# Squared-ReLU attention and a two-layer MLP on one core: fewer and longer attention bursts between the MLP's matmuls

## Chip, core and metric

The kernel runs on one NeuronCore of a Trainium2 chip. The metric is the time of one execution on the device in microseconds. The profile is one execution taken by the hardware profiler. TensorE (PE) does the matrix products, ScalarE (ACT) and VectorE (DVE) read what it leaves in PSUM, GpSimd (POOL) casts inputs, SyncE (SP) issues most of the transfers.

## What is computed

There are 8 batches and 12 heads, with 448 rows and 64 columns per head. The inputs are float32.

```python
scores = (1 / sqrt(64)) * (q @ k.T)              # per batch and head
attn = maximum(scores, 0) ** 2 / 448
x = (attn @ v)  # heads side by side: 3584 rows of 768
h = x @ w_in                                      # 768 x 2048
g = maximum(h, 0) + alpha * minimum(h, 0)
out = g @ w_out                                   # 2048 x 768, float32
```

## The kernel before

**Quads and chunks.** The attention is cut into 24 quads, one for four heads of one batch: quads 3b to 3b+2 belong to batch b. The 448 keys of a quad are cut into 7 chunks (j = 0 to 6). For one chunk `scores` (L182) issues four matmuls on 64x64 tiles of the array, which run side by side, and a relu that takes the result from PSUM to a bf16 tile. `squares` (L206) or, for two chunks at a time in the first three quads, `squares2` (L196) squares it on VectorE. `attnv` (L218) multiplies the seven squared chunks of a quad by v, 28 matmuls on 64x64 tiles that add up in PSUM, and then copies the sum, scaled, to `xT`.

**MLP.** For each batch there are a first layer, `ffn1` (L255), of 16 units `ff`, six matmuls of 128x128 tiles each, and a second layer, `ffn2` (L273). A unit of the first layer is evacuated in two steps, `neg` on ScalarE (L269) and `gT` on VectorE (L270). A unit of the second layer is 16 matmuls in two halves, a copy on VectorE (L286), and for every second unit a store on SP's queue (L292). An even batch has 12 half units of the second layer, an odd one 16.

**PSUM.** `sc_ps` has two buffers of two banks for scores and A@V, `mm_ps` four of one bank, for the MLP, and for a burst's first chunk when it is given `mm_ps`.

**Order.** `manual_schedule` keeps the order in which the code issues instructions on each engine, so the written order is the schedule. Attention is not a stage of its own: while TensorE does the MLP of batch b, bursts of attention of later batches are put between its matmuls. Quads 0 to 2 come first; 3 to 5 are put by hand into batch 0's layers (the lists given to `play`, L468 to L476); 6 to 23 form one `stream` (L487) of chunks and A@V, cut into parts of three units, which `spread` (L345) puts at even distances between whole units of the first layer and half units of the second. `group` (L319) issues a part: A@V goes last, the first of three chunks uses `mm_ps` and either relus on ScalarE alone ("act2", in the first layer) or one half on each of ScalarE and VectorE ("both"). The A@V of a quad comes after chunk 1 of the next.

**Inputs.** With chunk 0 of quad n the group issues the loads of quad n+2 (`load`, L86) and the transposes of quad n+1 by DMA (`transpose`, L127), all on SP's queue; with chunk 4, the casts of quad n+2 to bf16 on POOL (`to_bf16`, L110). `raw`, `cast` and `qkT` have two buffers each, `o` three.

Of the kernel before, what the change touches and what calls it, by code (L numbers as in the profile page):

```python
# [20 lines left out]
NJ = 7  # L21
# [3 lines left out]
def kernel(  # L25
# [22 lines left out]
    def pool(name, bufs, **kw):  # L48
        return ctx.enter_context(tc.tile_pool(name=name, bufs=bufs, **kw))
# [5 lines left out]
    v_pool = pool("vp", 4)  # L55
    early_pool = pool("early", 2)
    qkT_pool = pool("qkT", 2)
    rl_pool = pool("rl", 3)
    at_pool = pool("at", 10)
    rl2_pool = pool("rl2", 3)  # L60
    at2_pool = pool("at2", 6)
    xT_pool = pool("xT", 2)
    g_pool = pool("g", 1)
    neg_pool = pool("neg", 3)
# [101 lines left out]
        else:  # L166
            nc.vector.tensor_scalar(rl[:, r], half[r][:, :S], 0.0, None, ALU.max)  # L167

    rl2, pairs = [], []

    def relu_tile(pair):

        if not pair:
            return rl_pool.tile([128, 2, S], BF16, tag="rl", name="rl")
        if not rl2:
            t = rl2_pool.tile([128, 2, 2, S], BF16, tag="rl2", name="rlp")
            rl2.extend([t, t])
            pairs.append(t)
        t = rl2.pop()
        return t[:, 1 - len(rl2)]  # L180

    def scores(n, j, relu="act", space=sc_ps, pair=False):  # L182

        ps, half = score_tile(space)
        score_mm(n, j, half)
        rl = relu_tile(pair)
        if relu in ("both", "act2"):
            relu_half(rl, half, 0, nc.scalar)
            relu_half(rl, half, 1, nc.vector if relu == "both" else nc.scalar)
        elif relu == "dve":  # L190
            nc.vector.tensor_scalar(rl, ps[:, :, :S], 0.0, None, ALU.max)
        else:
            nc.scalar.activation(rl, ps[:, :, :S], ACTF.Relu)  # L193
        todo.append((n, j, rl))

    def squares2(keep=0):  # L196

        while len(todo) >= 2 + keep:
            two = [todo.pop(0) for _ in range(2)]
            t = pairs.pop(0)  # L200
            a = at2_pool.tile([128, 2, 2, S], BF16, tag="at2", name="atp")
            nc.vector.tensor_tensor(a, t, t, ALU.mult)  # L202
            for i, (n, j, _) in enumerate(two):
                att[(n, j)] = a[:, i]

    def squares(keep=0, eng=None):  # L206
        while len(todo) > keep:
            n, j, rl = todo.pop(0)
            a = at_pool.tile([128, 2, S], BF16, tag="at", name="at")
            if eng is nc.scalar:  # L210
                nc.scalar.activation(a, rl, ACTF.Square)
            else:
                nc.vector.tensor_tensor(a, rl, rl, ALU.mult)  # L213
            att[(n, j)] = a

    av_ps = {}

    def attnv(n, js=range(NJ), space=sc_ps, apart=False):  # L218
        b, g = quads[n]
        if js[0] == 0:  # L220
            if space is mm_ps:
                av_ps[n] = [mm_ps.tile([128, 512], F32, tag="mm", name="avh") for _ in range(2)]
            elif apart:
                av_ps[n] = [sc_ps.tile([128, 2, 512], F32, tag="sc", name="av2")[:, 0] for _ in range(2)]
            else:
                av_ps[n] = sc_ps.tile([128, 2, 512], F32, tag="sc", name="av")
        ps = av_ps[n]
        half = ps if isinstance(ps, list) else [ps[:, r] for r in range(2)]
        for j in js:
            a = att.pop((n, j))  # L230
            for r in range(2):
                for s in range(2):
                    nc.tensor.matmul(half[r][64 * s:64 * s + 64, :S],  # L233
                                     vb[n][64 * r:64 * r + 64, s, j, :],
                                     a[64 * r:64 * r + 64, s],
                                     start=(j == 0), stop=(j == NJ - 1))
        if js[-1] != NJ - 1:
            return
        if g == 0:
            xT[b] = xT_pool.tile([128, NG, 2, S], BF16, tag="xT", name="xT")  # L240
        if b == 0:
            nc.scalar.activation(xT[b][:, g, 0], half[0][:, :S], ACTF.Copy, scale=out_scale)
            if g > 0:
                nc.vector.tensor_scalar(xT[b][:, g, 1], half[1][:, :S], out_scale, None, ALU.mult)
            else:
                nc.scalar.activation(xT[b][:, g, 1], half[1][:, :S], ACTF.Copy, scale=out_scale)
        else:
            nc.scalar.activation(xT[b][:, g], ps[:, :, :S], ACTF.Copy, scale=out_scale)  # L248

# [69 lines left out]
    def group(units, how="both"):  # L319

        def f():
            order = sorted(units, key=lambda u: u[1] == "av")
            for i, (n, j) in enumerate(order):
                if j == "av":
                    attnv(n)
                elif i == 0 and len(order) == 3:
                    scores(n, j, how, mm_ps)
                else:
                    scores(n, j)
            squares()  # L330
            for n, j in order:
                if n < n_pe:
                    continue
                if j == 0:
                    if n + 2 < NQ:
                        load(n + 2)
                    if n + 1 < NQ:
                        transpose(n + 1, "k")
                        transpose(n + 1, "q")
                if j == 4 and n > 2 * NG and n + 2 < NQ:  # L340
                    for w in "kqv":
                        to_bf16(n + 2, w, nc.gpsimd)
        return f

    def spread(seq, items, share=0.92):  # L345

        total = sum(x[0] for x in seq) * share
        done, n = 0.0, 0
        for cost, fn in seq:
            while n < len(items) and done >= total * n / len(items):  # L350
                items[n]()
                n += 1
            fn()
            done += cost
        assert n == len(items)


    warm_w = singles.tile([128, 128], BF16)
# [34 lines left out]
    transpose(0, "k", first, nc.scalar)  # L393
    warm(2)
    nc.vector.tensor_copy(cast[(0, "k")][:, :, 3:], raw[(0, "k")][:, :, 3:])
    scores(0, 0, pair=True)
    scores(0, 1, pair=True)
    scores(0, 2, "both", mm_ps, pair=True)
    transpose(0, "k", rest)
    ps = mm_ps.tile([128, KF], F32, tag="mm", name="aps")  # L400
    nc.tensor.transpose(ps, alpha_sb, ident_f)
    nc.vector.tensor_scalar(beta_sb, ps, -1.0, 1.0, ALU.mult, ALU.add)
    squares2(keep=1)
    for n in range(NG):
        last = n == NG - 1
        for j in range(NJ):
            if n == 0 and j < 3:
                continue
            if last and j == 6:
                scores(n, j)  # L410
                squares2()
            elif j == 5 and not last or j == 2:
                scores(n, j, "both", mm_ps, pair=True)
            else:
                scores(n, j, "dve" if last and j == 4 else "act", pair=True)
            if not (last and j == 6):
                squares2(keep=1)
            if j == 2 and n > 0:
                attnv(n - 1, space=mm_ps)
            if j == 3 and not last:  # L420
# [17 lines left out]
    nc.gpsimd.dma_start(out=w_out_sb[:, :, :384], in_=w_out_v[:, :, :384])  # L438
    load_bf16(4)
    nc.gpsimd.dma_start(out=w_out_sb[:, :, 384:], in_=w_out_v[:, :, 384:])  # L440
    squares(eng=nc.scalar)
    attnv(2, range(0, 4), apart=True)
    attnv(2, range(4, NJ))
    ffn1(0, 3, range(0, 4))
# [12 lines left out]
    def play(seq):  # L457
        for x in seq:
            x()

    def g(*units):
        return group([(int(u[0]), "av" if u[1:] == "a" else int(u[1:])) for u in units])


    for ff in range(4):
# [5 lines left out]
    load(6, after=w_out_sb[:, 0, 384:385])  # L471
    load(7)
    o = [lambda c=c, hf=hf, h=h: ffn2(0, c, hf, h) for hf in range(2) for c in range(3) for h in range(2)]
    play([g("36"), turn(4), o[0], o[1], g("40", "41", "3a"), o[2], o[3], g("42", "43", "44"), o[4], o[5],
          g("45", "46"), o[6], turn(5), o[7], g("50", "51", "4a"), feed(6, "k", "q"), o[8], o[9],
          g("52", "53", "54"), feed(6, "v"), o[10], g("55", "56"), feed(7, "k", "q"), o[11]])  # L476

    ffn1(1, 0, range(0, 4))
    ffn1(1, 1, range(0, 4))
# [4 lines left out]
        ffn1(1, ff, range(4, KM))  # L484


    stream = []  # L487
    for n in range(2 * NG, NQ):
        for j in range(NJ):
            stream.append((n, j))  # L490
            if j == 1 and n > 2 * NG:
                stream.append((n - 1, "av"))
    stream.append((NQ - 1, "av"))
    parts = [stream[:2]] + [stream[i:i + 3] for i in range(2, len(stream), 3)]

    count = 0
    for b in range(1, B - 1):
        n_in, n_out = ((2, 7 if b == 1 else 6) if b % 2 else (3, 5))
        if b == B - 2:
            n_out = len(parts) - count - n_in  # L500
        mlp = steps(b, "in")
        bursts = [group(x, "act2") for x in parts[count:count + n_in]]
        if b == 1:
            bursts.append(lambda: [to_bf16(2 * NG + 2, w, nc.gpsimd) for w in "kqv"])
        spread(mlp[3:] if b == 1 else mlp, bursts, 0.95)
        count += n_in
        spread(steps(b, "out"), [group(x) for x in parts[count:count + n_out]], 0.92)
        count += n_out
    for _, fn in steps(B - 1, "in") + steps(B - 1, "out")[:-4]:
        fn()  # L510
    ffn2_last(B // 2 - 1, NJ - 1)
# [30 lines left out]
```

## Time and profile before

| | us |
|---|---|
| median of 9 runs | 396.9 (396.08 to 398.68) |
| the profiled execution | 396.34 |
| its span, first to last instruction | 394.5 |
| TensorE busy with matmuls | 384.0 |
| VectorE busy | 256.5 |
| ScalarE busy | 220.4 |
| GpSimd busy | 71.9 |
| mean granted clock of TensorE | 0.996 |

Two kinds of lines of the profile are used below. A line of a group has: kernel line, engine, operation, tiles (out<-in) with shapes, count | busy us, mean ns of one | idle time before it and what ended it. A line of the timeline has: start in us from the begin of the span, time to the end of the last of the merged instructions, engine, kernel line, operation, tiles and count. The end of a matmul in it is modelled and laps over the start of the next, so rates are read from start to start. In square brackets stands idle time of the engine ahead of the line and what ended it.

### The profile page before, as it was taken

What the parts mean: (1) busy time and instruction counts of PE and PEld (TensorE: products, weight loads), DVE (VectorE), ACT (ScalarE), POOL (GpSimd) and SP (SyncE); (2) the same over time, 40 slices, a digit from 0 to 9 for tenths busy, and PEclk for the clock granted to TensorE, in tenths of its full rate; (3) what the DMA queues carried; (4) which work ended last, traced back from release to release, by engine and by line L of the source; (5) the groups of instructions that cost most, each with busy time, mean ns of one, the idle gap of its engine ahead of it and who ended that gap; (6) DMA issues with size and microseconds to landing.
All of it is one profiled execution on the core that took longest, in us unless ns stands there. A gap on an engine that the chain in (4) does not pass through costs nothing.

```text
span 394.5 us, 7951 instructions
## 1 busy us (share of the span) xinstructions
PE 384.0 (97%) x3210; PEld 201.6 (51%) x3210; DVE 256.5 (65%) x406; ACT 220.4 (56%) x345; POOL 71.9 (18%) x88
## 2 busy tenths in 40 slices
PE   6799999999999999999999999999999999999996
PEld 4344555445555455544555455554555545555564
DVE  3966965676675877577664877667575776735421
ACT  5966847674655674466553765646454575624200
POOL 5654000022031430042020350033002300000000
PEclk9989999999999999999999999999999999999999
DMA  7999998592579923492097962295058720130033
GB/s 158 181 209 204 205 216 274 128 310 37 150 132 213 298 86 88 123 284 47 2 218 216 252 178 47 75 265 154 2 155 177 206 47 2 42 80 2 0 81 80
DMA packets 64756, 55.44 MB, mean 141 GB/s; under 512 B 35776, under 2 KB 60496, under 8 KB 64720
## 3 DMA queue, kind: packets, MB, share of 16 engines
q1 hardware_dynamic: 53472, 44.77, 44.8%
q0 software_dynamic: 10976, 9.96, 15.9%
q8 instruction: 25, 0.41, 0.4%
q10 hardware_dynamic: 272, 0.21, 0.2%
q14 instruction: 11, 0.09, 0.1%
HBM read 45.62 MB, written 11.01 MB: 144 GB/s over the span
## 4 chain that ended last, share of the span: by engine, by line
PE 92%; DVE 3%; ACT 2%; DMA 1%; issue 1%; ACTq 0%; DVEq 0%
PE ops L278 36%; PE hps L262 36%; PE av L233 8%; PE sc L158 5%; PE sch L158 4%; PE ops L301 1%; DVE atp L202 1%; ACT rlp L193 1%; DMA qraw<-in_q_dram 1%; PE tps L133 1%; DVE at L213 1%; PE avh L233 1%; ACT rl L193 0%; DVE gT L270 0%; ACT xT L248 0%
## 5 line engine op out<-in xcount | busy, mean ns | idle before, releaser
L262 PE MATMUL hps<-xT,w_in_sb 128*128 128x448 bf16 x768 | 150.1, 353 | 0.5 <-DVE gT L270 0.2
L278 PE MATMUL ops<-w_out_sb,gT 128*128 128x384 bf16 x864 | 147.9, 327 | 0.0
L278 PEld LDWEIGHTS <-gT 128*128 128x128 bf16 x864 | 81.1, 98 | 64.9 <-issue 14.2
L262 PEld LDWEIGHTS <-w_in_sb 128*128 128x128 bf16 x768 | 73.2, 98 | 74.5 <-issue 8.9
L213 DVE TENSOR_TENSOR at<-rl 128x896 bf16<-128x896 bf16 x147 | 97.8, 684 | 18.1 <-ACT rl L193 7.6
L270 DVE SCALAR_TENSOR_TENSOR gT<-neg,beta_sb,hps 128x448 bf16<-128x448 f32 x128 | 84.0, 677 | 36.7 <-ACT neg L269 36.5
L269 ACT ACTIVATE neg<-hps 128x448 f32<-128x448 f32 x128 | 68.5, 553 | 56.6 <-PE hps L262 54.5
L193 ACT ACTIVATE rl<-sc 128x896 bf16<-128x896 f32 x95 | 83.3, 926 | 1.7 <-PE sc L158 1.7
L165 ACT ACTIVATE rl<-sch 128x448 bf16<-128x448 f32 x67 | 34.8, 543 | 76.2 <-PE sch L158 76.2
L286 DVE COPY osb<-ops 128x384 f32<-128x384 f32 x54 | 30.0, 555 | 51.5 <-PE ops L278 51.5
L108 POOL CAST kb<-kraw 128x896 bf16<-128x896 f32 x16 | 16.5, 1031 | 207.2 <-DMA kraw<-in_k_dram 199.8
L158 PE MATMUL sc<-qT,kT 64*64 64x448 bf16 x440 | 33.8, 354 | 3.5 <-ACT rlp L193 1.8
L167 DVE TENSOR_SCALAR rl<-sch 128x448 bf16<-128x448 f32 x39 | 24.2, 621 | 15.4 <-PE sch L158 15.4
L233 PE MATMUL av<-at,vb 64*64 64x448 bf16 x592 | 32.0, 349 | 0.0
L158 PEld LDWEIGHTS <-kT 64*64 64x64 bf16 x672 | 14.9, 106 | 28.5 <-issue 22.5
L233 PEld LDWEIGHTS <-vb 64*64 64x64 bf16 x672 | 20.7, 110 | 13.8 <-issue 1.8
L248 ACT ACTIVATE xT<-av 128x896 bf16<-128x896 f32 x21 | 19.4, 922 | 7.4 <-PE av L233 7.3
L158 PE MATMUL sch<-qT,kT 64*64 64x448 bf16 x232 | 22.5, 376 | 0.0
L108 POOL CAST vb<-vraw 128x896 bf16<-128x896 f32 x16 | 17.4, 1089 | 0.0
L108 POOL CAST qb<-qraw 128x896 bf16<-128x896 f32 x16 | 17.4, 1085 | 0.0
L193 ACT ACTIVATE rlp<-sc 128x896 bf16<-128x896 f32 x14 | 12.3, 931 | 1.2 <-PE sc L158 1.2
L202 DVE TENSOR_TENSOR atp<-rlp 128x1792 bf16<-128x1792 bf16 x10 | 10.8, 1089 | 0.7 <-ACT rlp L193 0.3
(56 smaller groups left out, 87.9 us busy)
## 6 DMA issues: line engine op xcount, KB each, us to landing
out_dram<-osb SPq DMA_DIRECT2D x54, 192.0 KB, 2.8
qraw<-in_q_dram SPq DMA_DIRECT2D x19, 448.0 KB, 4.6
kraw<-in_k_dram SPq DMA_DIRECT2D x18, 448.0 KB, 5.4
vraw<-in_v_dram SPq DMA_DIRECT2D x18, 448.0 KB, 6.2
w_out_sb<-in_moe_w_out_dram POOLq DMA_DIRECT2D x2, 1536.0 KB, 21.2
w_in_sb<-in_moe_w_in_dram POOLq DMA_DIRECT2D x8, 192.0 KB, 8.5
w_in_sb<-in_moe_w_in_dram POOLq DMA_DIRECT2D x4, 384.0 KB, 9.9
vb<-in_v_dram POOLq DMA_DIRECT2D x6, 224.0 KB, 9.3
```

The costliest lines, as they stand in the source:

```text
L108: eng.tensor_copy(o, i)
L158: nc.tensor.matmul(half[r][64 * c:64 * c + 64, :S], kT[n][64 * r:64 * r + 64, j, c, :], qT[n][64 * r:64 * r + 64, :, c, :], start=True, st ...
L165: nc.scalar.activation(rl[:, r], half[r][:, :S], ACTF.Relu)
L167: nc.vector.tensor_scalar(rl[:, r], half[r][:, :S], 0.0, None, ALU.max)
L193: nc.scalar.activation(rl, ps[:, :, :S], ACTF.Relu)
L213: nc.vector.tensor_tensor(a, rl, rl, ALU.mult)
L233: nc.tensor.matmul(half[r][64 * s:64 * s + 64, :S], vb[n][64 * r:64 * r + 64, s, j, :], a[64 * r:64 * r + 64, s], start=(j == 0), stop=(j ...
L262: nc.tensor.matmul(ps, w_in_sb[:, km // 2, km % 2, bass.ts(ff, 128)], xT[b][:, km // 2, km % 2, :], start=(km == 0), stop=(km == KM - 1))
L269: nc.scalar.activation(neg, ps, ACTF.Relu, scale=-1.0)
L270: nc.vector.scalar_tensor_tensor(gT[b // 2][:, ff, (b % 2) * S:(b % 2) * S + S], neg, beta_sb[:, ff:ff + 1], ps, ALU.mult, ALU.add)
L278: nc.tensor.matmul(ps, gT[sb][:, ff, bass.ts(c, 128)], w_out_sb[:, ff, bass.ts(hf, 384)], start=(ff == 0), stop=(ff == KF - 1))
L286: nc.vector.tensor_copy(o[:, bass.ts(hf, 384)], ps)
```

## The change

For quads 6 to 23, `stream`, `parts` and `spread` are replaced by two bursts for each quad at written-out steps: `first_half` has chunks 0 to 2, `second_half` chunks 3 and 4, the A@V of the preceding quad on two `mm_ps` banks, and chunks 5 and 6. The steps count half units: in the first layer 32 of three matmuls (a burst at an odd step stands inside the accumulation of a unit), and then those of the second layer from step 32 on. Quad 6 has its chunks 3 to 6 in two bursts of two (`two`). For quads 3 to 5 the list behind `o` gets groups of three and two `wrap`s (two chunks, A@V, two chunks). All squares are of two chunks at a time, on tiles of `rl` (four buffers) and `at` (eight), but for the last chunk of a quad or stage. The sum of an A@V on `mm_ps` goes half to ScalarE and half to VectorE. `feed_next` issues the casts of quad n+1 and its transposes after the first half of quad n, and the loads of n+2 stay with that half.

```diff
-    def squares(keep=0, eng=None):
-        while len(todo) > keep:
...
+    def squares(keep=0, single=None):
+        while len(todo) >= 2 + keep or todo and single is not None:
+            m = min(len(todo), 2)
+            some = [todo.pop(0) for _ in range(m)]
+            t = some[0][2]
+            a = at_pool.tile([128, 2, 2, S], BF16, tag="at", name="at")
+            if m == 2:
+                nc.vector.tensor_tensor(a, t, t, ALU.mult)
...
+        elif isinstance(ps, list):
+            nc.scalar.activation(xT[b][:, g, 0], half[0][:, :S], ACTF.Copy, scale=out_scale)
+            nc.vector.tensor_scalar(xT[b][:, g, 1], half[1][:, :S], out_scale, None, ALU.mult)
...
+    def wrap(before, n, after):
+        def f():
+            scores(n + 1, before, "act")
+            scores(n + 1, before + 1, "dve")
+            attnv(n, space=mm_ps)
+            scores(n + 1, after, "act")
+            scores(n + 1, after + 1, "act")
+            squares()
+        return f
...
-    play([g("36"), turn(4), o[0], o[1], g("40", "41", "3a"), o[2], o[3], g("42", "43", "44"), o[4], o[5],
-          g("45", "46"), o[6], turn(5), o[7], g("50", "51", "4a"), feed(6, "k", "q"), o[8], o[9],
-          g("52", "53", "54"), feed(6, "v"), o[10], g("55", "56"), feed(7, "k", "q"), o[11]])
+    play([o[0], turn(4), o[1], g("36", "40", "41"), o[2], o[3], wrap(2, 3, 4), o[4], turn(5), o[5],
+          g("46", "50", "51"), o[6], o[7], wrap(2, 4, 4), feed(6, "k", "q"), o[8], o[9], g("56"), flush, feed(6, "v"), feed(7, "k", "q"), o[10], o[11]])
...
+    def first_half(n):
+        scores(n, 0, "act2", mm_ps)
+        scores(n, 1, "dve")
+        scores(n, 2, "act")
+        squares()
+        if n + 2 < NQ:
+            load(n + 2)
+        if n == 2 * NG:
+            transpose(n + 1, "k")
+            transpose(n + 1, "q")
+
+    def second_half(n):
+        scores(n, 3, "act")
+        scores(n, 4, "dve")
+        attnv(n - 1, space=mm_ps)
+        scores(n, 5, "act")
+        scores(n, 6, "act")
+        squares(keep=1)
...
+    def feed_next(n, w):
+        if n + 1 < NQ:
+            to_bf16(n + 1, w, nc.vector if w == None else nc.scalar if w == None else nc.gpsimd)
+            if w != "v":
+                transpose(n + 1, w)
...
+    STEPS = {1: [9, 17, 25, 33, 36, 38, 41, 43, 46], 0: [9, 23, 33, 35, 38, 41], 2: [9, 23, 33, 36, 40, 44]}
     for b in range(1, B - 1):
...
+        lo, hi = (2 * NG if b == 1 else 3 * b + 4), min(3 * b + 7, NQ)
+        where = STEPS[1] if b == 1 else STEPS[2 * (b % 2)]
+        items = [(n, f) for n in range(lo, hi) for f in (first_half, second_half)]
+        if b == 1:
+            items[1:2] = [(2 * NG, two(2 * NG, 3)), (2 * NG, two(2 * NG, 5, True))]
...
+            if f is first_half and n > 2 * NG:
+                for d, w in zip((2,4,6) if s < 32 else (0,0,1), "kqv"):
+                    at.setdefault(s + d, []).append(lambda n=n, w=w: feed_next(n, w))
+            if f is second_half:
+                for d, sq in zip((3,5) if s < 32 else (0,0), (squares, flush)):
+                    at.setdefault(s + d, []).append(sq)
         if b == B - 2:
+            at.setdefault(where[len(items)], []).append(lambda: attnv(NQ - 1))
```

More of the change, by code (lines that the diff above doesn't have):

```diff
@@ L57 @@
     qkT_pool = pool("qkT", 2)
[L58 to L61, printed above, removed]
+    rl_pool = pool("rl", 4)
+    at_pool = pool("at", 8)
     xT_pool = pool("xT", 2)
@@ L167, in relu_half, with scores @@
             nc.vector.tensor_scalar(rl[:, r], half[r][:, :S], 0.0, None, ALU.max)
[L169 to L182, printed above, removed]
-        ps, half = score_tile(space)
-        score_mm(n, j, half)
-        rl = relu_tile(pair)
+    cur = []
+    def scores(n, j, relu="act", space=sc_ps, rs=range(2)):
+        ps, half = score_tile(space)
+        score_mm(n, j, half, rs)
+        if cur:
+            t, i = cur.pop(), 1
+        else:
+            t, i = rl_pool.tile([128, 2, 2, S], BF16, tag="rl", name="rl"), 0
+            cur.append(t)
+        rl = t[:, i]
         if relu in ("both", "act2"):
@@ L193, in scores @@
             nc.scalar.activation(rl, ps[:, :, :S], ACTF.Relu)
[L194 to L203, printed above, removed]
-                att[(n, j)] = a[:, i]
-    def squares(keep=0, eng=None):
-        while len(todo) > keep:
[L208 to L214, printed above, removed]
+        todo.append((n, j, t))
+    def squares(keep=0, single=None):
[6 more added lines that the diff above has]
+                nc.vector.tensor_tensor(a, t, t, ALU.mult)
+            else:
+                cur.clear()
+                if single is nc.scalar:
+                    nc.scalar.activation(a[:, 0], t[:, 0], ACTF.Square)
+                else:
+                    nc.vector.tensor_tensor(a[:, 0], t[:, 0], t[:, 0], ALU.mult)
+            for i, (n, j, _) in enumerate(some):
+                att[(n, j)] = a[:, i]
     av_ps = {}
@@ L324, in f @@
                 if j == "av":
+                    if (n, NJ - 1) not in att:
+                        squares(single=nc.vector)
                     attnv(n)
@@ L343, in group @@
         return f
[L345 to L355, printed above, removed]
     warm_w = singles.tile([128, 128], BF16)
@@ L395 @@
     nc.vector.tensor_copy(cast[(0, "k")][:, :, 3:], raw[(0, "k")][:, :, 3:])
-    scores(0, 0, pair=True)
-    scores(0, 1, pair=True)
-    scores(0, 2, "both", mm_ps, pair=True)
+    scores(0, 0)
+    scores(0, 1)
+    scores(0, 2, "both", mm_ps)
     transpose(0, "k", rest)
@@ L402 @@
     nc.vector.tensor_scalar(beta_sb, ps, -1.0, 1.0, ALU.mult, ALU.add)
-    squares2(keep=1)
+    squares(keep=1)
     for n in range(NG):
@@ L410 @@
                 scores(n, j)
-                squares2()
+                squares()
             elif j == 5 and not last or j == 2:
-                scores(n, j, "both", mm_ps, pair=True)
+                scores(n, j, "both", mm_ps)
             else:
-                scores(n, j, "dve" if last and j == 4 else "act", pair=True)
+                scores(n, j, "dve" if last and j == 4 else "act")
             if not (last and j == 6):
-                squares2(keep=1)
+                squares(keep=1)
             if j == 2 and n > 0:
@@ L440 @@
     nc.gpsimd.dma_start(out=w_out_sb[:, :, 384:], in_=w_out_v[:, :, 384:])
-    squares(eng=nc.scalar)
+    squares(single=nc.scalar)
     attnv(2, range(0, 4), apart=True)
@@ L459, in play, with flush @@
             x()
+    def wrap(before, n, after):
[7 more added lines that the diff above has]
+        return f
     def g(*units):
         return group([(int(u[0]), "av" if u[1:] == "a" else int(u[1:])) for u in units])
+    def flush():
+        squares(single=nc.vector)
     for ff in range(4):
@@ L484 @@
         ffn1(1, ff, range(4, KM))
[L487 to L496, printed above, removed]
-    for b in range(1, B - 1):
-        n_in, n_out = ((2, 7 if b == 1 else 6) if b % 2 else (3, 5))
-        if b == B - 2:
[L500 to L508, printed above, removed]
+    def first_half(n):
+        scores(n, 0, "act2", mm_ps)
+        scores(n, 1, "dve")
+        scores(n, 2, "act")
+        squares()
+        if n + 2 < NQ:
[3 more added lines that the diff above has]
+            transpose(n + 1, "q")
@@ new lines, in second_half, with two, f @@
+    def second_half(n):
[4 more added lines that the diff above has]
+        scores(n, 6, "act")
+        squares(keep=1)
+    def two(n, j, last=False):
+        def f():
+            scores(n, j, "act2", mm_ps)
+            scores(n, j + 1, "act")
+            if last:
+                flush()
+            else:
+                squares()
+        return f
+    def feed_next(n, w):
[3 more added lines that the diff above has]
+                transpose(n + 1, w)
@@ new lines, in mlp_steps @@
+    def mlp_steps(b):
+        seq = [(0.56, h == 1, lambda ff=ff, h=h: ffn1(b, ff, range(3 * h, 3 * h + 3))) for ff in range(KF) for h in range(2)]
+        return seq + [(1.3, True, fn) for _, fn in steps(b, "out")]
+    STEPS = {1: [9, 17, 25, 33, 36, 38, 41, 43, 46], 0: [9, 23, 33, 35, 38, 41], 2: [9, 23, 33, 36, 40, 44]}
+    for b in range(1, B - 1):
+        mlp = mlp_steps(b)
+        at = {}
+        lo, hi = (2 * NG if b == 1 else 3 * b + 4), min(3 * b + 7, NQ)
[3 more added lines that the diff above has]
+            items[1:2] = [(2 * NG, two(2 * NG, 3)), (2 * NG, two(2 * NG, 5, True))]
+        for (n, f), s in zip(items, where):
+            at.setdefault(s, []).append(lambda n=n, f=f: f(n) if f in (first_half, second_half) else f())
+            if f is first_half and n > 2 * NG:
[4 more added lines that the diff above has]
+                    at.setdefault(s + d, []).append(sq)
+        if b == B - 2:
+            at.setdefault(where[len(items)], []).append(lambda: attnv(NQ - 1))
+        for i, (_, _, fn) in enumerate(mlp):
+            for x in at.pop(i, []):
+                x()
+            if b > 1 or i >= 6:
+                fn()
+        assert not at, at
```

## The prediction, made before the changed kernel ran

> **What bounds the kernel now.** I read the page's busy shares first, then the chain that ended last, then TensorE alone in order of time.
>
> ```profile
> PE 384.0 (97%) x3210; PEld 201.6 (51%) x3210; DVE 256.5 (65%) x406; ACT 220.4 (56%) x345; POOL 71.9 (18%) x88
> PE 92%; DVE 3%; ACT 2%; DMA 1%; issue 1%; ACTq 0%; DVEq 0%
> ```
>
> TensorE is busy 97% of the span and 92% of the last chain is its own work, with a granted clock of 0.996. An edit that leaves TensorE's instruction list alone can therefore gain only by the time between instructions. The timeline of TensorE shows where that is:
>
> ```profile
> 202.71 2.77 PE L278 MATMUL ops<-w_out_sb,gT 128*128 128x384 bf16 x16
> 205.41 0.38 PE L158 MATMUL sch<-qT,kT 64*64 64x448 bf16 x4
> 205.63 0.55 PE L158 MATMUL sc<-qT,kT 64*64 64x448 bf16 x8
> 206.11 4.07 PE L278 MATMUL ops<-w_out_sb,gT 128*128 128x384 bf16 x24
> 210.11 0.38 PE L158 MATMUL sch<-qT,kT 64*64 64x448 bf16 x4
> ```
>
> Column one is the start. 16 MLP matmuls take 205.41 - 202.71 = 2.70 us to the next start, 24 take 210.11 - 206.11 = 4.00: 0.1625 us each, and 0.10 us that is not matmul, at the edge into attention. The burst of three score chunks takes 206.11 - 205.41 = 0.70 us, where a further chunk costs 0.19 (205.63 to 206.11 holds two and the way out, and the seven chunks of an A@V run at the same 0.19): 3 x 0.19 = 0.57, so 0.13 us more. A burst of attention between MLP matmuls so costs **0.23 us** beside its work, whatever its length: the price of going from 128x128 to 64x64 tiles and back. It is no idle time in the profile; the modelled ends of the matmuls cover it.
>
> **The rule beside the row.** The Trainium skill's TensorEngine Tiling (Array Packing), Key Properties, says that changing the tiling mode drains TensorE, and gives no price; its TensorE: Matmul & The Clock Gate, Single matmul latency, puts the part of a warm matmul that isn't streaming at about 0.166 us. Two drains by that estimate are 0.33 us a burst; the trace has 0.23. I take the row. With 13 bursts fewer (below) the page would give -4.3 us and the row -3.0.
>
> **The change, part by part.**
>
> *Bursts.* Before, the written-out stream of quads 6 to 23 has 18 x 7 chunks and 18 A@V, 144 units: one part of 2 and 48 of up to 3, 49 bursts, which is what the timeline shows from 77.7 us on. After, STEPS places 9 bursts for batch 1, 6 in each of batches 2 to 5, 4 in batch 6 and one for the last A@V: 9 + 24 + 4 + 1 = 38. In the hand-made order of quads 3 to 5 behind `o`, score and A@V bursts go from 8 (four groups of three units, two of two, chunk 36 and the last A@V) to 6: two groups of three, two `wrap`s, chunk 56, the last A@V. The two `turn`s stay. 13 bursts x 0.23 = **-3.0 us**, all on the path. Matmuls and weights loaded are the same number.
>
> *A stall that goes.* In the stretch of quad 5, chunk 56 waits for a score buffer, since the cast of quad 6's v sits on ScalarE ahead of a relu:
>
> ```profile
> 70.52 0.95 ACT L106 CAST vb<-vraw 128x896 bf16<-128x896 f32 x1
> 70.70 0.38 PE L158 MATMUL sc<-qT,kT 64*64 64x448 bf16 x4 [0.15 <-ACT rl L193]
> ```
>
> Its start is 0.53 us after the chunk before it instead of 0.18. After, chunk 56 is alone and both buffers are free: **-0.35 us**. The wait for xT of quad 5 behind its A@V at 76 us stays.
>
> *Evacuation.* Squares: before 147 single ones and 10 pairs on VectorE; after 74 pairs and 19 singles.
>
> ```profile
> L213 DVE TENSOR_TENSOR at<-rl 128x896 bf16<-128x896 bf16 x147 | 97.8, 684 | 18.1 <-ACT rl L193 7.6
> L202 DVE TENSOR_TENSOR atp<-rlp 128x1792 bf16<-128x1792 bf16 x10 | 10.8, 1089 | 0.7 <-ACT rlp L193 0.3
> L191 DVE TENSOR_SCALAR rlp<-sc 128x896 bf16<-128x896 f32 x1 | 1.1, 1081 | 0.0
> ```
>
> 147 x 0.684 + 10 x 1.089 = 111.4 us becomes 74 x 1.089 + 19 x 0.684 = 93.6: -17.8. Relus: 39 half tiles at 0.621 leave VectorE, 4 of those stay, and 37 whole ones at 1.081 come (chunks 1 and 4 of the late quads, one per `wrap`): +18. Nineteen halves of xT at 0.62 come: +12. VectorE ends 12 us up, near 269 of 391 us; ScalarE loses some 28 us of its instructions. Both lie beside TensorE; this costs nothing as long as the burst doesn't wait for a PSUM buffer. That cover has to be worked out, for the Tiling page's PSUM Bottleneck speaks against the change: tiling speeds TensorE, not the evacuation, and the copies may become the bound. The paces, from a burst in the first MLP layer:
>
> ```profile
> 269.37 0.38 PE L158 MATMUL sch<-qT,kT 64*64 64x448 bf16 x4
> 269.48 0.54 ACT L269 ACTIVATE neg<-hps 128x448 f32<-128x448 f32 x1 [0.59 <-PE hps L262]
> 269.92 0.98 ACT L165 ACTIVATE rl<-sch 128x448 bf16<-128x448 f32 x2
> 270.06 0.68 DVE L270 SCALAR_TENSOR_TENSOR gT<-neg,beta_sb,hps 128x448 bf16<-128x448 f32 x1 [0.45 <-ACT neg L269]
> 270.77 1.75 ACT L193 ACTIVATE rl<-sc 128x896 bf16<-128x896 f32 x2
> ```
>
> ScalarE starts half tiles 0.44 us apart and whole ones 0.82; VectorE frees the last MLP bank 1.37 us after a burst begins (270.06 + 0.68 - 269.37). The new bursts of the first layer stand at odd steps, three matmuls (0.57 us) after the last full unit, so that one is free at 0.80.
>
> Second half at step 23, times from its first score: chunk 3 at 0, chunk 4 at 0.21, A@V 0.40 to 1.73, chunk 5 at 1.73, chunk 6 at 1.92, MLP again at 2.2. ScalarE: relu 3 0.42-1.35, half of xT 1.95-2.49, relus 5 and 6 to 4.1, then `neg` of the broken-off unit ff 11, 4.0-4.5. VectorE: gT of ff 10 to 0.80, relu 4 0.72-1.80, half of xT to 2.57, two pairs to 4.7, gT of ff 11 to 5.3. So chunk 5 has its buffer 0.35 us early and chunk 6 with about 0.06 us to spare (0.05 us from release to TensorE taken off): **0**, and 0.1 to 0.3 a burst if relu 4 is late. In the second layer VectorE has only a copy of 0.56 us ahead, and relu 4 starts at 0.65: more room. MLP banks: ff 12 (2.77) takes ff 10's (0.80), ff 13 (3.91) and ff 14 (5.04) the two of the A@V (2.5, 2.6), ff 15 (6.18) that of ff 11 (5.3): 0.9 us of room. First half at step 9: MLP again at 0.69; ff 5 to ff 7 take banks free at 0.80, 0.96 and 1.4, ff 8 (4.67) that of ff 4 (gT at 3.6): 1 us of room. This holds because the pool gives the bank that was freed first: in the compiled program of before, after the burst at 316.11 us ff 6 has ff 4's bank, ff 7 the first score half's, and only ff 8 that of ff 5.
>
> I add **+0.3 us** for waits that this leaves, chiefly at the first burst of quad 6, close behind three units that finish together; its bounds are 0 and 2. Below nothing is excluded.
>
> *Queues.* `feed_next` casts quad n+1 on POOL and issues its two transposes on SP behind the loads of n+2; before, the casts came with chunk 4, for n+2. No instruction is added. SP's order stays loads, transposes, stores.
>
> ```profile
> kT<-kb SPq DMA_TRANSPOSE x18, 5.5
> qT<-qb SPq DMA_TRANSPOSE x18, 4.8
> ```
>
> A transpose waits for the last score of the quad two back, and a store behind it on SP waits with it. The tightest case is quad 9 in batch 1: its transposes can go when quad 7's second half (step 36) is over and the loads of quad 10 are issued, some 3.4 us after that burst began, and land some 8.5 us later (as those issued at 212.4 and landed at 222.7 us did): at 12; its first chunk (step 43) is at about 15, by 7 MLP steps of 1.3 and bursts of 2.45, 1.0 and 2.45. Cost **0** with 3 us of room; without it TensorE would wait the difference. Stores held some 5 us have three buffers, each 5.2 us of work.
>
> *Squares against POOL.* The only bank wait of the late part of before is this:
>
> ```profile
> 309.67 3.43 DVE L213 TENSOR_TENSOR at<-rl 128x896 bf16<-128x896 bf16 x3 [0.76 <-ACT rl L165]
> 310.04 1.33 POOL L108 CAST qb<-qraw 128x896 bf16<-128x896 f32 x1
> 311.31 1.32 POOL L108 CAST vb<-vraw 128x896 bf16<-128x896 f32 x1
> PE hps L262 <- DVE gT L270: 0.2, 1, 0.2
> ```
>
> Three squares beside POOL's casts took 3.43 us, where three of 0.62 are usual; gT came late and ff 4 began 0.26 us late, at 313.75. With batch 5's burst elsewhere: -0.26 there, which I hold against new ones of the kind (first rival) and count as 0.
>
> Sum: -3.0 - 0.35 + 0.3 = -3.05 us. The profiled execution, 396.34 us (span 394.5 and 1.8 around it), becomes 393.3, its span 391.4. It lies 0.56 under the median 396.9, so the median becomes 393.8; with the 0.26 it would be 393.6. I say **393.7**.
>
> **Rivals.**
> *Squares late beside POOL.* A pair beside casts may take 2.4 us (1.09 x 1.34 / 0.62). In a second half of the first layer two such put gT of ff 11 at 7.9 against 6.18: 1.7 us lost, at 5 places; in a first half 0.3 at 6. Two full meetings cancel the gain; all would be 5 x 1.7 + 6 x 0.3 = 10. For it: raw loads issued at the start of a batch land 6 us later, so casts fall into the first layer. Against: casts fill 72 of 394 us and before lost 0.26 in all. About half of the meetings at half price: 395.5 to 397.5. Chance 0.13.
> *Banks come back in turn.* Slower: if the pool handed out banks in rotation, ff 6 behind a first half would need ff 4's bank, whose `neg` sits behind three relus: 3.6 + 0.05 - 2.4 = 1.3 us at each of 13 first-layer bursts, +17, less 3: 410. It decides from 0.25 us a burst. The addresses quoted speak against it. Chance 0.04.
> *Transposes late.* If SP is held longer than 3 us, quads 8 to 12 each wait 1 to 2 us: about 398. Chance 0.04.
> *It doesn't remove the switches' cost.* If TensorE pays inside a longer burst (scores, A@V, scores) what it saves at its edges: 396.5. Against: at 201.28 us A@V follows scores without a gap. Chance 0.03.
>
> **The numbers.** Forecast 0.76. Over 0.2% (0.8 us, about what a measurement of this kernel can tell from no change) faster: the forecast and a third of the first rival, 0.81; same 0.07; slower 0.12. Range: 392.2 (the page's drain, the 0.26 and 0.3 less waiting) to 396.3 (half the first rival).
>
> **What would show it.** After: 13 fewer 64x64 runs with 0.23 us each way of edge still on each; TensorE's idle time before `hps` and `sc` in the late part under 1 us; atp-like pairs near 1.09; VectorE near 269, ScalarE near 192-200 us. It is wrong if waits of `hps` for gT, or of `sc` for a relu on VectorE, add up to over 2 us, or scores wait for kT.

## The result and the profile after

| | before | changed |
|---|---|---|
| median, us | 397.0 (31 runs, 396.0 to 398.9) | 392.7 (10 runs, 392.1 to 394.2) |
| ratio of times | | 0.9888, 95% interval 0.9873 to 0.9903 |
| profiled execution, its span, us | 396.34, 394.5 | 392.68, 390.9 |
| mean granted clock of TensorE in that execution | 0.996 | 0.999 |
| forecast, us | | 393.7 (392.2 to 396.3) |

The change makes the kernel faster by 4.3 us, 1.1%.

In the lines below `hps` is a unit of the first layer in PSUM and `ops` one of the second, `sc` and `sch` are scores, `av` and `avh` the sum of an A@V, and `tps` is a transpose on TensorE. From the page of the changed kernel, the busy shares and the chain that ended last, then VectorE's groups for squares and whole relus, then TensorE's waits for `gT`:

```profile
PE 379.3 (97%) x3210; PEld 203.7 (52%) x3210; DVE 274.6 (70%) x363; ACT 197.6 (51%) x314; POOL 75.3 (19%) x88
PE 89%; DMA 7%; DVE 1%; POOL 1%; issue 0%; ACT 0%; POOLq 0%
L196 DVE TENSOR_TENSOR at<-rl 128x1792 bf16<-128x1792 bf16 x74 | 85.7, 1183 | 5.7 <-ACT rl L185 2.1
L183 DVE TENSOR_SCALAR rl<-sc 128x896 bf16<-128x896 f32 x38 | 41.4, 1089 | 8.6 <-PE sc L156 8.6
L202 DVE TENSOR_TENSOR at<-rl 128x896 bf16<-128x896 bf16 x19 | 14.6, 770 | 0.9 <-ACT rl L185 0.9
PE hps L255 <- DVE gT L263: 0.4, 2, 0.2
```

TensorE still has its 3210 matmuls and is still busy 97% of the span, but "busy" fell from 384.0 to 379.3 us. Some of that is the start, which differs from one execution to the next (a second profile of before has 383.0). From the end of quad 3's transposes on, where the work is the same and the granted clock is 1.00 in all three, TensorE is busy for 354.8 and 355.0 us in the two profiles of before and for 351.9 in the changed kernel: some 3 us of what counted as busy was the change of tile size. VectorE went up by 18 us and ScalarE down by 23, off the path. One of the two waits for `gT` in the last line is in the start, at 29 us; the other is at 278 us. The DMA in the chain is the start's too and no work of the change: the second profile of before also has 4% of it.

The timeline of TensorE, around one second half in the second layer:

```profile
206.74 0.65 PE L271 MATMUL ops<-w_out_sb,gT 128*128 128x384 bf16 x3
207.32 0.57 PE L156 MATMUL sc<-qT,kT 64*64 64x448 bf16 x8
207.73 1.49 PE L223 MATMUL avh<-at,vb 64*64 64x448 bf16 x28
209.05 0.55 PE L156 MATMUL sc<-qT,kT 64*64 64x448 bf16 x8
209.53 5.37 PE L271 MATMUL ops<-w_out_sb,gT 128*128 128x384 bf16 x32
214.74 0.92 PE L255 MATMUL hps<-xT,w_in_sb 128*128 128x448 bf16 x4
```

Between the pieces of the burst there is nothing: A@V takes 209.05 - 207.73 = 1.32 us, seven times 0.19, without the 0.10 of a way out that it had before:

```profile
201.28 1.49 PE L233 MATMUL av<-at,vb 64*64 64x448 bf16 x28
```

The next start there is 202.71 (the prediction shows that line), so A@V and its way out took 1.43 us. In the changed kernel the four chunks and the A@V take 2.21 us for 2.08 of work, so one pair of edges serves 11 chunk-sized pieces. And 32 MLP matmuls run to the next start without attention, 5.21 us: 32 x 0.1625 is 5.20. That next start belongs to the other layer, with other operands but on the same 128x128 tiles, and it costs nothing either; the time goes where the tile size changes.

To place the 4.3 us I cut the span at two points of TensorE's timeline: the first `hps` after quad 3's transposes (the first cut), and the first `hps` of batch 1 (the second). Two lines from the profile of before, then two from that of the changed kernel:

```profile
35.55 2.44 PE L262 MATMUL hps<-xT,w_in_sb 128*128 128x448 bf16 x12
72.33 1.68 PE L262 MATMUL hps<-xT,w_in_sb 128*128 128x448 bf16 x8
34.96 2.44 PE L255 MATMUL hps<-xT,w_in_sb 128*128 128x448 bf16 x12
71.04 1.68 PE L255 MATMUL hps<-xT,w_in_sb 128*128 128x448 bf16 x8
```

| us | start | quads 3 to 5 | rest |
|---|---|---|---|
| before, profile shown above | 35.55 | 36.78 | 322.2 |
| before, second profile | 35.19 | 36.78 | 322.7 |
| changed | 34.96 | 36.08 | 319.9 |

The start has the same instructions in the same order in all three. It took 34.7 to 36.3 us in the changed kernel and in the six of the kernels below that leave it alone, so 34.96 against 35.55 and 35.19 is no sign that the change shortened it. What holds it up differs as well. In the first profile of before the granted clock was 0.78 from 16 to 22 us and 0.93 from 22 to 28, and TensorE did not wait for quad 3's loads at its transposes; in the second, at 1.00, it sat idle before them for 1.03 and 0.55 us, and in the changed kernel for 0.69 and 0.55.

### The profile page after: what moved, and what is told of

It reads as the page before. It is cut to its first block, busy times and chain, and to the rows that moved or that the text cites. A ratio compares the mean times of both kernels' runs of the same rounds, so it can differ in the third digit from the quotient of the medians.

```text
span 390.9 us, 7785 instructions
## 1 busy us (share of the span) xinstructions
PE 379.3 (97%) x3210; PEld 203.7 (52%) x3210; DVE 274.6 (70%) x363; ACT 197.6 (51%) x314; POOL 75.3 (19%) x88
## 4 chain that ended last, share of the span: by engine, by line
PE 89%; DMA 7%; DVE 1%; POOL 1%; issue 0%; ACT 0%; POOLq 0%
PE ops L271 37%; PE hps L255 34%; PE sc L156 6%; PE avh L223 6%; DMA qe<-in_q_dram 3%; DMA w_in_sb<-in_moe_w_in_dram 2%; PE sch L156 2%; DMA vb<-in_v_dram 2%; PE ops L294 1%; DVE at L196 1%; PE av L223 1%; DMA alpha_sb<-in_moe_alpha_dram 1%; PE tps L131 1%; ACT xT L241 0%; POOL ke L367 0%
## 5 line engine op out<-in xcount | busy, mean ns | idle before, releaser
L185 ACT ACTIVATE rl<-sc 128x896 bf16<-128x896 f32 x101 | 89.7, 923 | 39.9 <-PE sc L156 39.9
L262 ACT ACTIVATE neg<-hps 128x448 f32<-128x448 f32 x128 | 68.5, 548 | 77.7 <-PE hps L255 76.7
L196 DVE TENSOR_TENSOR at<-rl 128x1792 bf16<-128x1792 bf16 x74 | 85.7, 1183 | 5.7 <-ACT rl L185 2.1
L183 DVE TENSOR_SCALAR rl<-sc 128x896 bf16<-128x896 f32 x38 | 41.4, 1089 | 8.6 <-PE sc L156 8.6
L156 PE MATMUL sc<-qT,kT 64*64 64x448 bf16 x556 | 40.1, 354 | 3.6 <-ACT rl L185 1.6
L163 ACT ACTIVATE rl<-sch 128x448 bf16<-128x448 f32 x49 | 24.6, 545 | 26.7 <-PE sch L156 26.7
L223 PE MATMUL avh<-at,vb 64*64 64x448 bf16 x588 | 31.8, 349 | 0.6 <-DVE at L196 0.6
L238 ACT ACTIVATE xT<-avh 128x448 bf16<-128x448 f32 x19 | 10.3, 543 | 11.0 <-PE avh L223 11.0
L202 DVE TENSOR_TENSOR at<-rl 128x896 bf16<-128x896 bf16 x19 | 14.6, 770 | 0.9 <-ACT rl L185 0.9
L239 DVE TENSOR_SCALAR xT<-avh 128x448 bf16<-128x448 f32 x19 | 11.9, 625 | 4.5 <-PE avh L223 4.5
L156 PE MATMUL sch<-qT,kT 64*64 64x448 bf16 x116 | 11.2, 370 | 0.0
## 6 DMA issues: line engine op xcount, KB each, us to landing
w_in_sb<-in_moe_w_in_dram POOLq DMA_DIRECT2D x4, 384.0 KB, 9.8
```

Source lines behind the costliest of these rows:

```text
L156: nc.tensor.matmul(half[r][64 * c:64 * c + 64, :S], kT[n][64 * r:64 * r + 64, j, c, :], qT[n][64 * r:64 * r + 64, :, c, :], start=True, st ...
L163: nc.scalar.activation(rl[:, r], half[r][:, :S], ACTF.Relu)
L223: nc.tensor.matmul(half[r][64 * s:64 * s + 64, :S], vb[n][64 * r:64 * r + 64, s, j, :], a[64 * r:64 * r + 64, s], start=(j == 0), stop=(j ...
L262: nc.scalar.activation(neg, ps, ACTF.Relu, scale=-1.0)
```

## Experiments

**The late part back in 49 bursts.** In place of the two halves, with quads 3 to 5 and the pair squares as changed (the old times of loads, casts and transposes and the undivided copy of an A@V's sum come back with the old parts):

```diff
-    def first_half(n):
...
-    STEPS = {1: [9, 17, 25, ...
...
+    stream = []
+    for n in range(2 * NG, NQ):
+        for j in range(NJ):
...
+        spread(mlp[3:] if b == 1 else mlp, bursts, 0.95)
```

> The changed kernel with the late part (quads 6 to 23) put back into the old parts of up to three units, spread as before: 49 bursts there instead of 38. The new order of quads 3 to 5 and the squares of two chunks stay. Theory of the edges (each burst between MLP matmuls costs 0.23 us, whatever it holds): 11 x 0.23 = 2.5 us slower than the changed kernel, so about 395.2 us, and TensorE shows no more idle time than before. Rival, relief (the gain comes from fewer VectorE and ScalarE instructions, paired squares above all): the paired squares are still there, so it stays within 0.5 us of the changed kernel, 392.7 to 393.2.

Measured: 399.33 us, ratio to before 1.0061 (1.0042 to 1.0079). Both theories missed it: it is 6.6 us above the changed kernel and slower than before. Timeline of all engines around an A@V:

```profile
118.15 1.09 DVE L196 TENSOR_TENSOR at<-rl 128x1792 bf16<-128x1792 bf16 x1
119.16 0.62 DVE L202 TENSOR_TENSOR at<-rl 128x896 bf16<-128x896 bf16 x1
119.30 0.38 PE L223 MATMUL av<-at,vb 64*64 64x448 bf16 x4 [0.63 <-DVE at L196]
```

The last four matmuls of the A@V start 0.98 us after those before them and not 0.18: chunk 6 had been left without a partner, and its square was issued as half of a pair only in the burst of its own A@V. TensorE waits for such a pair five times, 0.8 us lost each.

**The same, with the quad's squares finished early.**

```diff
             squares()
+            if any(n >= n_pe and j == NJ - 1 for n, j in order):
+                squares(single=nc.vector)
```

> The kernel with the late part in the old 49 bursts, and in addition the squares of a quad are finished with the part that holds its last chunk, a single square if need be. Without that, five A@V waited 0.63 us idle (0.82 from start to start) for a pair square issued only in their own burst. If those five waits are the whole excess over the edges, they go and the time is 399.3 - 5 x 0.82 = 395.2 us, 11 x 0.23 above the changed kernel. If the old parts cost more for another reason, it stays above 396.5.

Measured: 395.29 us, ratio to before 0.9960 (0.9945 to 0.9975). The five waits are gone and 4.0 us with them. What is left over the changed kernel is 2.6 us, where 11 bursts of 0.23 make 2.5. So pair squares alone, in the old parts, lose; with the squares of a quad closed in time they are free of charge, and no gain either: from batch 1 on this profile takes 322.8 us, as before did with single squares (322.2 and 322.7).

**Each second half in two bursts.**

```diff
         attnv(n - 1, space=mm_ps)
+        squares(keep=1)
+
+    def rest_of(n):
         scores(n, 5, "act")
         scores(n, 6, "act")
...
+                at.setdefault(s + 1, []).append(lambda n=n: rest_of(n))
```

> The changed kernel with each second half of a quad cut into two bursts, chunks 3 and 4 with the A@V, and chunks 5 and 6 one step later: 17 more bursts, the same instructions otherwise. Edges: 17 x 0.23 = 3.9 us slower than the changed kernel, about 396.6, each burst with about 0.10 us on the way in and 0.13 on the way out. Relief: evacuation has more time between the pieces, so no slower than 392.7. If TensorE paid inside a long burst what it saves at the edges (third rival of the prediction), also 392.7.

Measured: 396.60 us (12 runs), 3.9 above the changed kernel; ratio to before 0.9987 (0.9976 to 0.9999). TensorE's timeline:

```profile
210.04 1.49 PE L223 MATMUL avh<-at,vb 64*64 64x448 bf16 x28
211.47 1.47 PE L271 MATMUL ops<-w_out_sb,gT 128*128 128x384 bf16 x8
212.88 0.57 PE L156 MATMUL sc<-qT,kT 64*64 64x448 bf16 x8
213.38 2.94 PE L271 MATMUL ops<-w_out_sb,gT 128*128 128x384 bf16 x17
```

A@V is back at 1.43 us, eight MLP matmuls take 1.41 for 1.30, two chunks 0.50 for 0.38: 0.33 us in these three rows, of which one way out, 0.10, was there in the single burst too. The waits of `hps` for `gT` went away in the late part, and still the time rose by what the edges cost. VectorE (363) and ScalarE (314) have as many instructions as in the changed kernel. That refutes the reading that the gain is relief of VectorE and ScalarE, and the rival that a long burst pays inside what it saves outside.

**Bursts of the first layer between whole units.**

```diff
-    STEPS = {1: [9, 17, 25, ...], 0: [9, 23, ...], 2: [9, 23, ...]}
+    STEPS = {1: [10, 18, 26, ...], 0: [10, 24, ...], 2: [10, 24, ...]}
```

> The changed kernel with the bursts of the first layer one step later, between whole units (steps 10 and 24, in batch 1 also 18 and 26), instead of three matmuls into a unit. Theory of the margin: gT of the unit just ended holds VectorE until 1.37 us after the burst begins, so the relu of chunk 4 runs from 1.29 to 2.37 and chunk 6, wanted at 1.92, waits about 0.5 us at each of 5 second halves: 2.5 us slower, about 395.2, as idle time before sc released by the VectorE relu. Rival (the broken-off unit is what costs, since its evacuation waits behind the burst's relus): 0.3 to 0.5 us faster, about 392.3, and the wait of hps for gT is gone.

Measured: 395.06 us, 2.3 above the changed kernel; ratio to before 0.9946 (0.9928 to 0.9965). Timeline of one second half that begins at 274.13, and TensorE's waits:

```profile
274.81 0.68 DVE L263 SCALAR_TENSOR_TENSOR gT<-neg,beta_sb,hps 128x448 bf16<-128x448 f32 x1 [0.46 <-ACT neg L262]
275.41 1.08 DVE L183 TENSOR_SCALAR rl<-sc 128x896 bf16<-128x896 f32 x1
276.55 0.38 PE L156 MATMUL sc<-qT,kT 64*64 64x448 bf16 x4 [0.33 <-DVE rl L183]
PE sc L156 <- DVE rl L183: 1.7, 5, 0.3
```

`gT` of the unit just ended ends at 275.49, the relu of chunk 4 runs from 1.28 to 2.36 us of the burst, and chunk 6 starts at 2.42 instead of 1.92: 0.50 us lost (the profile calls 0.33 of it idle, since the matmul before is modelled to last longer), at the 5 second halves, 2.5 us. The odd step is what makes the burst of four fit. The theory gave 395.2 us. The rival's point is seen too, in size far behind: the late `hps` waits for `gT` are gone, some 0.3 us.

**Squares one chunk at a time in quads 6 to 23.**

```diff
-            if m == 2:
+            if m == 2 and some[0][0] >= n_pe:
+                for i in range(2):
+                    nc.vector.tensor_tensor(a[:, i], t[:, i], t[:, i], ALU.mult)
+            elif m == 2:
```

> The changed kernel with the squares of quads 6 to 23 issued one chunk at a time on the same tiles: 54 pairs become 108 single ones. Edges: VectorE is busy some 10 us more (108 x 0.684 - 54 x 1.18) and the time stays at 392.7, up to +0.5 where squares meet POOL's casts. Relief: the paired squares are part of the gain, 1 us or more slower, over 393.7.

Measured: 393.74 us, 1.0 above the changed kernel, ratio to before 0.9913 (0.9892 to 0.9933); VectorE 278.5 us. By the numbers set down, this is relief's side, by a hair; the runs go from 392.6 to 394.5 us. So with long bursts the pairs are worth about 1 us. The timeline shows where:

```profile
182.65 4.22 DVE L197 TENSOR_TENSOR at<-rl 128x896 bf16<-128x896 bf16 x4
184.54 1.32 POOL L106 CAST vb<-vraw 128x896 bf16<-128x896 f32 x1
187.52 0.73 PE L258 MATMUL hps<-xT,w_in_sb 128*128 128x448 bf16 x3 [1.03 <-DVE gT L266]
```

Four squares beside POOL's casts took 4.22 us; three `gT` came late behind them and `hps` lost 1.2 us there and 0.45 at 279 us. At a place of the same kind in the changed kernel the same work, two pairs, takes 3.38 us (below). From batch 1 on this profile is 1.3 us longer than that of the changed kernel (which loses 0.03 and 0.35 us at these places), and these two waits are all of it: the pair matters where it meets POOL, and nowhere else.

**The casts on ScalarE instead of POOL.** In `feed_next`, `nc.gpsimd` becomes `nc.scalar`.

> The changed kernel with the casts of quads 8 to 23 on ScalarE instead of POOL. If POOL's casts are what stretches the pair squares (mean 1183 ns, up to 1.8 us, where 1.09 is usual) and makes hps wait 0.35 us for gT: pairs back at 1.09, no such wait, 392.4 us. Rival: on ScalarE the casts run in program order, behind the relus of a first half, so the transposes of the next quad start some 4 us after it and land some 10 us after it, as late as the next first half at 9.9: scores wait for kT or qT, up to 2 us at some of 11 first halves of the second layer, and the time is 393 to 400.

Measured: 393.64 us, ratio to before 0.9928 (0.9905 to 0.9951), so no gain. Pair squares of its page, and the timeline of a second half that begins at 150.71:

```profile
L196 DVE TENSOR_TENSOR at<-rl 128x1792 bf16<-128x1792 bf16 x74 | 78.9, 1087 | 5.7 <-ACT rl L185 2.2
151.06 0.96 ACT L104 CAST vb<-vraw 128x896 bf16<-128x896 f32 x1
151.90 0.94 ACT L185 ACTIVATE rl<-sc 128x896 bf16<-128x896 f32 x1
152.89 0.57 PE L156 MATMUL sc<-qT,kT 64*64 64x448 bf16 x8 [0.28 <-ACT rl L185]
```

The first half of the expectation holds: with POOL out, pairs take 1087 ns on average instead of 1183, and no late `hps` waits for `gT`. The casts now stand ahead of the relu of chunk 3, and chunk 5 waits for its buffer, 0.45 us at two places. The time from the first cut on is 0.6 us longer than in the changed kernel; this profile also has a start of 36.3 us, longer than any other, which the edit doesn't explain. The rival's 393 to 400 us holds the result, but for another reason than it gave: no score waits for `kT` or `qT`, so the transposes were in time.

**Two small edits aimed at what is left.**

```diff
-            load_w_in(1024, 2048)
             load_bf16(3)
+            load_w_in(1024, 2048)
...
-    STEPS = {1: [9, 17, 25, ...
+    STEPS = {1: [11, 19, 25, ...
```

> The changed kernel with two small edits: quad 3's loads are issued ahead of the last third of w_in, since its transposes wait about 1.2 us idle for them at 33 us; and batch 1's first two bursts stand at steps 11 and 19 instead of 9 and 17, away from the three units that finish together (0.27 us lost at 78 us). If the start is held by these loads, 1.2 to 1.6 us earlier from there on and 0.2 from the second: 391.0 to 391.5. If w_in is late then instead, hps waits for it at 36 to 40 us, and the time is 392.5 or more.

Measured: 392.39 us, ratio to before 0.9882 (0.9864 to 0.9900): inside the interval of the changed kernel. First TensorE's timeline of the changed kernel, then that of this one:

```profile
33.32 0.58 PE L131 MATMUL tps<-ident,ke 128*64 128x128 bf16 x14 [0.69 <-DMA ke<-in_k_dram]
34.45 0.58 PE L131 MATMUL tps<-ident,qe 128*64 128x128 bf16 x14 [0.55 <-DMA qe<-in_q_dram]
```

```profile
32.94 0.58 PE L131 MATMUL tps<-ident,ke 128*64 128x128 bf16 x14
36.05 1.10 PE L255 MATMUL hps<-xT,w_in_sb 128*128 128x448 bf16 x5 [0.70 <-DMA w_in_sb<-in_moe_w_in_dram]
```

The transposes no longer wait, and w_in does. With either order TensorE waits for what comes last; of 1.1 us won there 0.9 is lost 2 us later and 0.4 at quad 5's transposes. The wait at batch 1's first burst went, 0.13 us, but behind the third, at 88.75 us, `hps` came 0.18 late, so this edit gained nothing either.

**Before, a second profile.**

> The kernel before, unchanged, for a second profile of it. The 10 runs of the changed kernel gained 4.3 us on the median of before, but the two profiled executions differ by only 3.6 us in span, of which 3.0 lie after the transposes of quad 3 (from 35.5 us on in before, from 35.0 on in the changed kernel). If the rest is the start (loads of the first quads and the clock), this profile has the same 359.0 us from there on, and its start is longer than 35.5 us by what its time is over 396.3. If it is in the late part, the late part is longer than 359.0.

Its one time is 396.54 us, its start 35.19 us and the remainder 359.5, where the first profile has 359.0. VectorE's squares and TensorE at the same place as the wait shown in the prediction:

```profile
309.67 3.62 DVE L213 TENSOR_TENSOR at<-rl 128x896 bf16<-128x896 bf16 x3 [0.76 <-ACT rl L165]
313.94 1.29 PE L262 MATMUL hps<-xT,w_in_sb 128*128 128x448 bf16 x6 [0.29 <-DVE gT L270]
```

The wait of `hps` is 0.45 us here (0.26 in the first profile), and there is one more of 0.29 at 264 us: together they make 0.5 of the 0.56 us by which this remainder is longer. POOL's casts begin when the loads have landed (kb's was released by the landing of kraw), so this loss differs from run to run. The expectation had the missing time in the start or in the late part; the late part is longer, the start is shorter, and the median of before, 397.0, is still half a microsecond above both profiles.

## Why the prediction was right

*Edges.* The cost and the reason were right. The three counts of late bursts, 38, 49 and 55, gave 392.7, 395.3 and 396.6 us: 0.23 us for each of the 11 and of the 17 bursts more. By the single profiles from batch 1 on (319.9, 322.8 and 323.4 us) it is 0.26 and 0.21, since these also differ by some tenths of waits for `gT`. The row was the right price; the estimate from the Trainium skill's pages that the prediction names, 0.33, would have put the kernel with 55 at 398.3. What in a change of tile size takes the time (emptying the array, or the weights that come late) no run here separates.

*The stall at chunk 56 and quads 3 to 5.* Worked out -0.35 and two bursts, -0.81; measured 36.78 to 36.08, -0.70, and 36.08 again in every kernel here with the new order and the old loads. One of the two bursts was counted 0.10 too dear: chunk 36 stood right ahead of the transposes of `turn`, so its going saved only one edge, 0.12 us.

*Evacuation costs nothing.* The timetable of the second half held to some hundredths. Times in the first layer, in the profile of the changed kernel:

```profile
271.77 0.57 PE L156 MATMUL sc<-qT,kT 64*64 64x448 bf16 x8
271.89 0.68 DVE L263 SCALAR_TENSOR_TENSOR gT<-neg,beta_sb,hps 128x448 bf16<-128x448 f32 x1 [0.45 <-ACT neg L262]
272.49 1.08 DVE L183 TENSOR_SCALAR rl<-sc 128x896 bf16<-128x896 f32 x1
273.18 0.94 POOL L106 CAST kb<-kraw 128x896 bf16<-128x896 f32 x1 [3.70 <-DMA kraw<-in_k_dram]
273.50 0.55 PE L156 MATMUL sc<-qT,kT 64*64 64x448 bf16 x8
274.29 3.38 DVE L196 TENSOR_TENSOR at<-rl 128x1792 bf16<-128x1792 bf16 x2
274.93 1.80 POOL L106 CAST vb<-vraw 128x896 bf16<-128x896 f32 x1
277.59 1.26 DVE L263 SCALAR_TENSOR_TENSOR gT<-neg,beta_sb,hps 128x448 bf16<-128x448 f32 x2
278.32 0.73 PE L255 MATMUL hps<-xT,w_in_sb 128*128 128x448 bf16 x3 [0.19 <-DVE gT L263]
```

`gT` of the last whole unit ends at 0.80 us of the burst, relu 4 runs 0.72 to 1.80, chunk 5 starts at 1.73 and chunk 6 right behind, without a wait: all as worked out. The margin of 0.06 us fits the even steps too: 0.57 us later, chunk 6 lost 0.50. The copy out of PSUM, which the prediction took from the Trainium skill's TensorEngine Tiling (Array Packing), PSUM Bottleneck, as what speaks against the change, made a score inside a burst wait only in the kernels with even steps and with the casts on ScalarE; what it costs `hps` stands under *New waits*.

*Banks.* No wait of 1.3 us anywhere in the first layer, so the slower rival is out.

*Squares against POOL.* This rival came about on a small scale. In the second halves that begin at 271.8 us and at 180.4 us the pairs fell beside casts. The two pairs took 3.38 us instead of some 2.1, `gT` of the broken-off unit ended at 6.5 us of the burst where its bank was wanted at 6.2, and `hps` began 0.35 us late; the other place fell within the slack and lost 0.03. The price of a full meeting, 1.7 us, was too high because it took 2.4 us for a pair; the longest here is 1.82. The prediction also misread one line: the wait of 0.2 us in `PE hps L262 <- DVE gT L270: 0.2, 1, 0.2` is one in the start, at 31 us. The late one of 0.26 is right by the starts of the matmuls; the profile doesn't list it as idle.

*Transposes.* Those of quad 9 landed at 111.9 us, 12.6 after quad 7's second half began, and the first chunk came at 113.8: 1.9 us of room, where 3 were worked out.

*New waits.* Worked out +0.3; measured 0.35 at 278, 0.03 at 187 and 0.13 at 78 us. That is 0.51, but before has 0.26 and 0.74 us of the same kind in its two profiles, which I had set to no gain, so on balance this term is between +0.25 and -0.23, about nothing.

*VectorE* ended at 274.6 us and not 269: 74 pairs at 1183 ns, not 1089, are 7 us more by themselves.

*The size.* Forecast -3.2, measured -4.3 us (the interval of the ratio says 3.9 to 5.0). From the first cut to the end the profiles give -3.0 and -3.6 against the two of before, which is the forecast and its variable waits. The start adds 0.2 to 0.6, which the prediction left at nothing and no edit explains. The last half microsecond is a step of the prediction that did not hold: it took the changed kernel's profiled execution to lie 0.56 below its median, as before's did, and it lay at the median (392.68 against 392.72). Why before's two profiles lie below its median stays open. So the extra 1.1 us is not from the edges. The lower end of the range was added up wrongly as well: with the page's drain, the 0.26 and no waits the prediction's own terms give 396.9 - 4.3 - 0.35 - 0.26 = 392.0, not 392.2. The measured time lies above both.

## What to carry to other kernels

When TensorE is "busy" all along, look at starts, not at busy time: fit the time of runs of equal matmuls of two lengths. What is left over was here the price of changing the tile size, 0.23 us for each burst whatever its length. Then make bursts as long as the PSUM buffers and the two evacuating engines allow, and write the timetable of one burst; here its margin was 0.06 us, and moving the burst by three matmuls cost 0.5 us each time. When squares or other steps are paired, close the pair in time for its consumer, or the partner's lateness costs more than the pairing brings.

## What the runs showed that I had not expected

A square that runs beside POOL's casts is slower: up to 1.40 us for a single one in before, where 0.62 is usual, and up to 1.82 for a pair. In the changed kernel the 59 pairs that met no cast took 1.08 to 1.09 us, the 15 that met one 1.56 on average; with the casts on ScalarE all 74 took 1.08 to 1.09. The casts suffer as well: v's cast in the last timeline took 1.80 us, beside pairs, where 1.03 to 1.09 was the mean before. `gT` and the relus, which read PSUM, kept their 0.68 and 1.09 us beside casts (16 of the `gT` ran wholly beside one). Pairs lose less in all than singles: 3.38 us for four chunks against 4.22, at one such place each.
